# Half of the normalized gate half by a Strassen level on x in float16, with y's scaling and o's loads moved

## The chip, the cores and the metric

The kernel runs on one core of a Trainium2 chip. The metric is the time of one execution on the device in microseconds (us); lower is better. A core has five engines that run their own instruction streams and meet at semaphores: TensorE (PE, matrix products; PEld is its weight load), VectorE (DVE), ScalarE (ACT), GpSimd (POOL) and SyncE (SP), which here only issues DMAs. Matmul results go to eight banks of 128 x 512 float32, from which VectorE and ScalarE fetch them.

## The reference, cut to what matters

Two branches read the same x of 2048 tokens by 1024 and are mixed by a gate per token:

```python
qkv = (x @ wqkv)            # 1024 x 3072: 32 heads of 32, q, k and v
logits = q . k[pos - 2*w] * 32**-0.5      # w = 0..7, masked where pos - 2*w < 0
o = softmax(logits) . v[pos - 2*w]
a = o @ wo                  # 1024 x 1024
z = gelu(x @ w_in)          # 1024 x 3584, tanh form
z1, z2 = z[:, :1792], layernorm(z[:, 1792:])
b = (z1 * (w_sp @ z2 + b_sp)) @ w_out     # w_sp 2048 x 2048, w_out 1792 x 1024
g = sigmoid(x . gate_w)
out = g * a + (1 - g) * b
```

All inputs are bfloat16.

## The kernel before

Almost all of the on-chip memory is one arena, cut by hand into regions whose tenants follow one another. x is held transposed (`xT`, 1024 rows on 8 x 128 partitions, 2048 tokens). The long matrix products are TensorE's stream, in this order:

- x's first transposes and 11 tiles of z2. A z2 tile (`z2_block`, L332) is 128 tokens by one column block of 448 (`ZC`): eight matmuls (L339) into one bank, then a gelu on ScalarE that also sums each row (L345). z2 has 16 x 4 such tiles. Column block 3 carries one column more, x times gate_w, which a small copy on ScalarE takes to `gl_s` (L348).
- q, k and v (`qkv_tile`, L739), eight groups of four heads with 16 tiles each: eight matmuls of 384 columns, a copy on ScalarE into one of three staging slots (L742), and every four tiles three DMA stores to scratch in HBM (L747). Behind group 1 stand eight z2 tiles.
- The other z2 tiles. Between them ScalarE takes squares of finished z2 rows (L797, for the variance) and the row norms of w_sp (`row_norm`, L572: the sum of absolute values of 128 rows of 2048, loaded by `load_nat`, L569). Ten row norms are spread over the q/k/v groups, 13 us apart; six stand here. VectorE makes means and variances for four tiles at a time (`stats`, L622) and normalizes z2 in place (`norm`, L631), to float16.
- z1: 64 tiles of the same kind (L836, gelu L839), stored to scratch.
- The mixing product w_sp @ z2 in 16 groups (`g_group`), by one Strassen level: seven products of eight matmuls of 448 columns in float16 (L853) in place of eight products. The operands' sums and differences are made ahead by VectorE; the results are combined in three banks and in copies on ScalarE (`fork`, L875; `keep`, L863 and L865). Behind them come the product with z1 (L908), the norm of y (`y_norm`, L696), a power of two as scale (`y_power`, L701) and the scaling to float16 (`y_scale`, L709, VectorE), and a store of y to scratch (`store_y`, L652).
- o @ wo and y @ w_out, by one Strassen level each, and the gated sum.

Meanwhile VectorE computes the attention from the scratch copies of q, k and v, head group by head group: products (L362), folds (L366), the maximum over the eight positions (`soft_a`, L383), the exponentials on ScalarE (L387), and the sums with v (L402, L408). Each group's q and k are loaded by `load_qk` (L415), its v by `load_v` (L419), and its result o is stored by `store_o` (L423).

The order of all side work is written out when the program is built, by a planner. `Beat` holds an estimate of TensorE's time (`now`, advanced by `beat.run` with each matmul's columns) and of VectorE's (`vector`); `beat.at(t, fn)` issues `fn` into the engines' streams when `now` passes t, and the attention's steps are issued `lead` ahead of the time at which VectorE should reach them. In the mixing stage three lists take spare work: `beside_fork` and `beside_copy` at two places of ScalarE's stream in each group, and `behind_mult` on VectorE. The engines run each stream strictly in order, so a wait of one instruction holds what stands behind it.

SP issues the DMAs in the order of the program; a DMA whose source is not ready holds those behind it. When the last attention group is done, `attended` (L473) stores o, loads wo, takes o's norm (`o_norm`, L499), and plans the transposing loads of o (`plan_heads`, `load_heads`, L492), o's scale and the sums of wo. wo's own norm is taken in eleven chunks (`wo_norm`, L670), whose loads follow one another from ScalarE's queue, in the mixing stage.

## Time and profile before

| | |
|---|---|
| time, median of 3 runs | 679.54 us (678.07 to 680.69) |
| the profiled execution | 679.48 us |
| its span, first to last instruction | 677.7 us |
| TensorE busy | 670.1 us, 99% |
| VectorE busy | 537.5 us, 79% |
| ScalarE busy | 381.1 us, 56% |
| GpSimd busy | 15.5 us, 2% |
| granted TensorE clock, mean | 1.0 |

The stages of TensorE, from the timeline: first z2 tiles to 24.8 us, q/k/v to 203.5 (group 0 to 45.6), the other z2 tiles to 271.9, z1 to 369.2, mixing to 541, wo to 584, w_out to 677. VectorE's attention runs from 55.27 to about 464.

The lines of the profile are read as follows. A group line names a line of the kernel, the engine, the operation, output and input tiles and their shapes, the count, the busy time in us and the mean of one in ns, and, behind the last bar, the idle time just before these instructions with what ended most of it. A line of the waits gives the waiting engine and instruction, what released it, and then the total time, the number of waits and the longest. A line of the timeline gives the start, the duration, the engine, the line and the operation; a bracket at its end holds the wait before it.

### The profile page before, as it was taken

The page shows a single profiled execution, that of the slowest core. Times are in us where ns is not written, and L with a number is a line of the kernel's source. Part 1 is how long each engine was busy: PE and PEld are TensorE (multiplying, and loading weights), DVE is VectorE, ACT ScalarE, POOL GpSimd, SP SyncE. Part 2 cuts the span into 40 slices and gives each one's busy share as a digit, 9 for nine tenths or more (in the row PEclk, how much of TensorE's full clock was granted, in tenths as well). Part 3 has the DMA queues.
Part 4 walks back from the last instruction along what each step waited for, and adds up shares of the span by engine and source line. Part 5 has one row for each costly group of instructions (what it writes and reads, how often), then busy time and mean ns, then how long its engine had stood idle before and what let it go on. Part 6 is the DMA issues. An engine that isn't in the chain of part 4 may idle for free.

```text
span 677.7 us, 9532 instructions
## 1 busy us (share of the span) xinstructions
PE 670.1 (99%) x3587; PEld 392.5 (58%) x3587; DVE 537.5 (79%) x588; ACT 381.1 (56%) x714; POOL 15.5 (2%) x68
## 2 busy tenths in 40 slices
PE   8999999999999999999999999999899999999997
PEld 4568688888885555555555555555455544444443
DVE  1007799999999999999999999997369587954745
ACT  4334646455645985979953666667555574522121
POOL 0000000000000002010100000000000000000000
PEclk9999999999999999999999999999999999999999
DMA  8979869988879754267545555949966699485211
GB/s 233 179 151 281 222 163 289 236 221 219 199 195 241 231 191 175 83 204 251 169 158 176 138 133 148 270 109 248 250 161 164 166 235 251 78 172 144 59 62 63
DMA packets 230734, 123.92 MB, mean 183 GB/s; under 512 B 191008, under 2 KB 217248, under 8 KB 230688
## 3 DMA queue, kind: packets, MB, share of 16 engines
q1 hardware_dynamic: 229104, 121.21, 68.6%
q10 hardware_dynamic: 1584, 2.10, 0.9%
q8 instruction: 28, 0.46, 0.3%
q14 instruction: 18, 0.15, 0.1%
HBM read 63.97 MB, written 37.82 MB: 150 GB/s over the span
## 4 chain that ended last, share of the span: by engine, by line
PE 95%; DMA 2%; SPq 2%; ACT 0%; issue 0%; DVE 0%; ACTq 0%
PE ps L853 36%; PE ps L739 18%; PE ps L339 11%; PE ps L836 11%; PE sd L739 6%; PE seed L853 6%; PE sd L339 4%; PE sd L836 4%; SPq L492 1%; DMA o_d<-arena 1%; DMA arena<-in_B_w_in_dram 1%; DMA y_d<-arena 0%; ACT arena L670 0%; SPq L720 0%; DVE arena L1011 0%
## 5 line engine op out<-in xcount | busy, mean ns | idle before, releaser
L853 PE MATMUL ps<-arena 128*128 128x448 f16 (+1 forms) x1296 | 264.4, 363 | 1.9 <-ACT arena L865 1.9
L853 PEld LDWEIGHTS <-arena 128*128 128x128 f16 x1512 | 147.8, 98 | 156.8 <-issue 2.6
L739 PEld LDWEIGHTS <-arena 128*128 128x128 bf16 x1024 | 141.7, 138 | 24.9
L739 PE MATMUL ps<-arena 128*128 128x384 bf16 x768 | 130.0, 326 | 0.0
L362 DVE TENSOR_TENSOR arena<-arena 128x8192 bf16<-128x8192 bf16 x16 | 70.8, 4422 | 43.9 <-DMA arena<-k_d 43.6
L339 PE MATMUL ps<-arena 128*128 128x448 bf16 (+1 forms) x384 | 77.9, 357 | 0.8 <-DMA arena<-in_B_w_in_dram 0.8
L742 ACT CAST arena<-ps 128x384 bf16<-128x384 f32 x96 | 45.1, 481 | 58.7 <-PE ps L739 58.7
L339 PEld LDWEIGHTS <-arena 128*128 128x128 bf16 x512 | 50.3, 99 | 47.3 <-issue 2.0
L836 PEld LDWEIGHTS <-arena 128*128 128x128 bf16 x512 | 50.0, 98 | 46.6
L366 DVE TENSOR_TENSOR arena<-arena 128x4096 bf16<-128x4096 bf16 (+1 forms) x64 | 74.1, 1158 | 2.0
L836 PE MATMUL ps<-arena 128*128 128x448 bf16 x384 | 75.4, 352 | 0.0
L402 DVE TENSOR_TENSOR arena<-arena,att_A 128x8192 bf16<-128x8192 bf16 x16 | 70.7, 4421 | 0.2
L853 PE MATMUL seed<-arena 128*128 128x448 f16 (+1 forms) x216 | 47.8, 363 | 0.0
L739 PE MATMUL sd<-arena 128*128 128x384 bf16 x256 | 46.8, 326 | 0.0
L408 DVE TENSOR_TENSOR arena<-arena 128x4096 bf16<-128x4096 bf16 x16 | 36.6, 2289 | 0.3
L345 ACT ACTIVATE arena<-ps 128x448 bf16<-128x448 f32 x48 | 26.2, 554 | 17.6 <-PE ps L339 17.3
L572 ACT ACTIVATE arena<-arena 128x2048 bf16<-128x2048 bf16 x16 | 30.8, 1922 | 8.1 <-DMA arena<-in_B_w_sp_dram 8.1
L1075 ACT ACTIVATE arena<-ps,omr 128x512 f32<-128x512 f32 x24 | 16.5, 688 | 32.7 <-PE ps L853 32.7
L839 ACT ACTIVATE arena<-ps 128x448 bf16<-128x448 f32 x48 | 25.1, 557 | 17.1 <-PE ps L836 16.0
L865 ACT ACTIVATE arena<-ps,bt 128x448 f32<-128x448 f32 x32 | 20.3, 634 | 21.9 <-PE ps L853 20.0
L1011 DVE SCALAR_TENSOR_TENSOR arena<-seed,omr,arena 128x512 bf16<-128x512 f32 x8 | 6.0, 750 | 32.7 <-PE seed L853 32.7
L696 ACT ACTIVATE arena<-arena 128x896 bf16<-128x896 bf16 x32 | 30.3, 946 | 1.0 <-DVE arena L908 0.5
(136 smaller groups left out, 602.3 us busy)
## 6 DMA issues: line engine op xcount, KB each, us to landing
arena<-in_B_w_sp_dram SPq DMA_DIRECT2D x16, 512.0 KB, 6.1
arena<-k_d SPq DMA_DIRECT2D x8, 960.0 KB, 7.1
arena<-v_d SPq DMA_DIRECT2D x8, 960.0 KB, 5.3
z_d<-arena SPq DMA_DIRECT2D x16, 448.0 KB, 3.1
arena<-z_d SPq DMA_DIRECT2D x16, 448.0 KB, 4.0
y_d<-arena SPq DMA_DIRECT2D x16, 448.0 KB, 3.6
arena<-in_A_wqkv_dram SPq DMA_DIRECT2D x24, 256.0 KB, 5.6
arena<-in_B_w_in_dram SPq DMA_DIRECT2D x6, 896.0 KB, 5.8
```

What stands on the lines that cost most here:

```text
L339: nc.tensor.matmul(ps[:, 0:N], xT[:, kt, i * P:(i + 1) * P], w2[:, kt, ZC * c:ZC * c + N], start=(kt == 0), stop=(kt == KT - 1))
L345: nc.scalar.activation(z2[:, i, ZC * c:ZC * (c + 1)], ps[:, 0:ZC], ACT.Gelu_apprx_tanh, accum_out=s1[:, 4 * i + c:4 * i + c + 1])
L362: TT(prod.rearrange("p (w j c) -> p w j c", w=W, j=8, c=C), in0, in1, ALU.mult)
L366: return lambda: TT(pv[:, :, 0:n], pv[:, :, 0:n], pv[:, :, n:2 * n], ALU.add)
L402: TT(prod.rearrange("p (w j d h) -> p w j d h", w=W, j=8, d=DH, h=HG), in0, in1, ALU.mult)
L408: return [(4.4, mul), (2.3, lambda: TT(p3[:, 0:4, :], p3[:, 0:4, :], p3[:, 4:8, :], ALU.add)), (1.2, lambda: TT(p3[:, 0:2, :], p3[:, 0:2, ...
L572: nc.scalar.activation(waste, slot, ACT.Abs, accum_out=l1[:, a:a + 1])
L696: nc.scalar.activation(waste, g_ring[n % 4][:, r], ACT.Abs, accum_out=yl[:, k:k + 1])
L739: nc.tensor.matmul(ps[:, 0:3 * C].rearrange("p (t c) -> p t c", t=3), lhsT, wgt[:, :, kt, :], start=(kt == 0), stop=(kt == KT - 1))
L742: nc.scalar.copy(st[:, j % 4, :].rearrange("p (t d h) -> p t d h", t=3, h=HG), ps[:, 0:3 * C].rearrange("p (t h d) -> p t d h", t=3, h=HG))
L836: nc.tensor.matmul(ps[:, 0:512 if whole and kt == 0 else ZC], xT[:, kt, i * P:(i + 1) * P], _sub_ap(w1, kt * ZC, [[1, 512 if whole and kt ...
L853: nc.tensor.matmul(ps[:, 0:c1 - c0], w[:, k, :], v[:, k, c0:c1], start=(first and k == 0), stop=(k == K - 1), skip_group_check=True)
```

## The change

z2's column blocks 2 and 3 are no longer computed tile by tile. For each of eight units of 256 tokens (`Tokens`) and the 896 columns of these two blocks, `z2_group` computes 2 x 2 blocks of results by one Strassen level: seven products of four matmuls of 449 columns (128 tokens by 512 rows of x; the 449th column is gate_w's). Three results of products are kept on ScalarE (`z2_keep`), VectorE makes two sums of them and a bank, two gelus read banks at once, and the other two (`z2_late`) read the sums in the next group, behind its fifth product; GpSimd takes the gate's column from there. The last-named two gelus stand before the third keep on ScalarE.

The operands of these products have to be float16. x is converted in place, each unit by a power of two: VectorE sums its absolute values (`x_abs`), a matmul with ones adds the partitions (`x_scales`), and VectorE multiplies (`x_convert`) and makes sums and differences (`x_sums`). The sums of the first four units are taken before group 0 of q/k/v, those of the others inside it, and the second scale matmul stands behind the fourteenth tile of group 0. Groups 1 to 7 of q/k/v and all z1 tiles read the converted x; their copies and gelus undo the scale. w_in's blocks are loaded in quarters (`load_d`), normed and scaled on ScalarE (`d_norm`, `d_convert`), and subtracted on VectorE (`d_sum`).

The eight groups stand inside q/k/v group 3, ahead of tiles 0, 3, 6, 9, 12 and 14 and behind the last. Of the other z2 tiles, three stand behind group 0, two ahead of group 3 and sixteen behind group 7; the eight behind group 1 go.

Moved or resized beside it: thirteen early row norms in place of ten, issued 5.9 us apart from the end of group 3, into two slots and in place; two staging slots for q/k/v in place of three; the first group's q and k loaded in halves; the maximum in `soft_a` by three halvings; squares with each of the last 16 z2 tiles' rows, and means and variances for eight tiles at a time; wo's norm in the z1 stage. In the mixing stage y's scale power follows the first group of a unit and the scaling is done by ScalarE in the second one (`y_scale_beside`), in two halves. After the attention, o's loads are planned later and apart, wo's load behind the first of them, and wo's scaling and sums behind that.

```diff
-L1_EARLY = 10
+L1_EARLY = 13
...
-    stage_slots = [reg(R_OFF + 29952 + r * 1536, 1536).rearrange("p (j c) -> p j c", j=4) for r in range(3)]
+    stage_slots = [reg(R_OFF + 29952 + r * 1536, 1536).rearrange("p (j c) -> p j c", j=4) for r in range(2)]
...
+    def x_abs(u):
+        nc.vector.tensor_reduce(xl[:, u:u + 1], tokens[u].raw, AX.XY, ALU.add, apply_absolute_value=True)
+
+    def x_cast(u0, u1):
+        nc.vector.tensor_copy(rs_n[:, u0:u1], xl[:, u0:u1])
+
+    def powers(src, scale, inv):
+        nc.vector.tensor_scalar(scale, src, 2.0 ** -30, 2.0 ** -13, ALU.max, ALU.mult)
+        nc.vector.tensor_scalar(scale.bitcast(U32), scale.bitcast(U32), EXPO, EXPO, ALU.bitwise_and, ALU.bitwise_xor)
+        nc.vector.tensor_scalar(inv.bitcast(U32), scale.bitcast(U32), EXPO, EXPO, ALU.bitwise_and, ALU.bitwise_xor)
+        nc.vector.tensor_scalar(inv, inv, 0.5, None, ALU.mult)
+
+    def x_scales(u0, u1):
+        ps = psum.tile([P, 512], F32, name="ps", tag="ps")
+        nc.tensor.matmul(ps[:, 0:u1 - u0], rows_one, rs_n[:, u0:u1], start=True, stop=True)
+        powers(ps[:, 0:u1 - u0], xs[:, u0:u1], xinv[:, u0:u1])
+
+    def x_convert(u):
+        nc.vector.tensor_scalar(tokens[u].whole, tokens[u].raw, xs[:, u:u + 1], None, ALU.mult)
+
+    def x_sums(u):
+        v = tokens[u]
+        TT(v.s1, v.a21, v.a22, ALU.add)
+        a11, a21 = [a.rearrange("p (r k) t -> p r k t", r=2) for a in (v.a11, v.a21)]
+        TT(v.s3, a11, a21, ALU.subtract)
+        TT(v.s2, v.s1, v.a11, ALU.subtract)
+        TT(v.s4, v.a12, v.s2, ALU.subtract)
...
+    def load_d(q):
+        h, c = q // 2, 2 + q % 2
+        sync.dma_start(d_raw[:, q, :, 0:ZC], win_v[:, 4 * h:4 * h + 4, FH + ZC * c:FH + ZC * (c + 1)])
+
+    def d_norm(q):
+        nc.scalar.activation(x_waste, d_raw[:, q], ACT.Abs, accum_out=dl[:, q:q + 1])
+
+    def d_total():
+        nc.vector.tensor_reduce(dsc, dl, AX.X, ALU.add)
+        nc.vector.tensor_copy(rs_n[:, 8:9], dsc)
+        beat.on_vector(0.3)
+
+    def d_scale():
+        ps = psum.tile([P, 512], F32, name="ps", tag="ps")
+        nc.tensor.matmul(ps[:, 0:1], rows_one, rs_n[:, 8:9], start=True, stop=True)
+        powers(ps[:, 0:1], dsc, dinv)
+        nc.vector.tensor_scalar(zinv, xinv, dinv, None, ALU.mult)
+        beat.on_vector(0.9)
+
+    def d_convert(q):
+        nc.scalar.activation(d_h[:, q], d_raw[:, q], ACT.Copy, scale=dsc)
+
+    def d_sum(m):
+        out_, a, b = ((r1, m12, m11), (r3, m22, m12), (r2, m22, r1), (r4, m21, r2))[m]
+        TT(out_, a, b, ALU.subtract)
+        beat.on_vector(1.1)
...
+    def z2_keep(ps):
+        out = z2_snaps[z2_kept[0] % 5]
+        z2_kept[0] += 1
+        nc.scalar.copy(out, ps[:, 0:DN - 1])
+        return out
+
+    def z2_product(ps, w, v, first):
+        for k in range(4):
+            lhsT = w[:, k // 2, k % 2, :] if len(w.shape) == 4 else w[:, k, :]
+            nc.tensor.matmul(ps[:, 0:DN - 1], lhsT, v[:, k, 0:DN - 1], start=(first and k == 0), stop=(k == 3),
+                             skip_group_check=True)
+        beat.run(4 * (DN - 1))
+
+    def z2_late(i, src, scale):
+        z2_out(src[:, 0:ZC], i, 3, scale)
+        nc.gpsimd.tensor_scalar(gl_s[:, i:i + 1], src[:, ZC:ZC + 1], scale, None, ALU.mult)
+
+    z2_wait = []
+
+    def z2_group(u):
+        v = tokens[u]
+        scale = zinv[:, u:u + 1]
+        pa, pd = [psum.tile([P, 512], F32, name="ps", tag="ps") for _ in range(2)]
+        z2_product(pa, v.a11, m11, True)
+        pb = seeded.tile([P, 512], F32, name="seed", tag="sd")
+        nc.scalar.copy(pb[:, 0:DN - 1], pa[:, 0:DN - 1])
+        z2_product(pd, v.s1, r1, True)
+        p5 = z2_keep(pd)
+        z2_product(pa, v.s2, r2, False)
+        u2 = z2_keep(pa)
+        z2_product(pb, v.a12, m21, False)
+        z2_out(pb[:, 0:ZC], 2 * u, 2, scale)
+        z2_product(pa, v.s3, r3, False)
+        while z2_wait:
+            z2_late(*z2_wait.pop(0))
+        u3 = z2_keep(pa)
+        TT(p5, p5, u3, ALU.add)
+        z2_product(pd, v.s4, m22, False)
+        TT(u2, u2, pd[:, 0:DN - 1], ALU.add)
+        beat.on_vector(1.3)
+        z2_product(pa, v.a22, r4, False)
+        z2_out(pa[:, 0:ZC], 2 * u + 1, 2, scale)
+        z2_wait.extend([(2 * u + 1, p5, scale), (2 * u, u2, scale)])
...
-        nc.vector.tensor_reduce(att_m[:, :, 0, :], L[:].rearrange("p (a w n) -> p a n w", a=2, w=W), AX.X, ALU.max)
+        TT(att_m[:], L4[:, :, 0:4, :], L4[:, :, 4:8, :], ALU.max)
+        TT(att_m[:, :, 0:2, :], att_m[:, :, 0:2, :], att_m[:, :, 2:4, :], ALU.max)
+        TT(att_m[:, :, 0:1, :], att_m[:, :, 0:1, :], att_m[:, :, 1:2, :], ALU.max)
...
         store_o(NG - 1)
-        load_wo()
         o_norm(NG - 1, reg(A_OFF + 8192, 2048).rearrange("p (j c) -> p j c", j=NJ))
         prep["attended"] = True
         t = max(beat.now, beat.vector)
-        plan_heads(0, t + 5.0, 3.0)
-        plan_heads(1, t + 11.0, 3.0)
-        beat.at(t + 5.0, o_total)
+        plan_heads(0, t + 7.0, 3.0)
+        beat.at(t + 10.5, load_wo)
+        plan_heads(1, t + 16.0, 3.0)
+        beat.at(t + 6.0, o_total)
         behind_mult.append((t + 14.0, 0.0, o_matmul))
         behind_mult.append((t + 15.0, 0.9, o_power))
+        behind_mult.append((t + 18.0, 2.45, lambda: heads_sums(0)))
         for m in range(4):
-            behind_mult.append((t + 10.0, 0.75, lambda m=m: wo_scale(m)))
-        behind_mult.append((t + 13.5, 2.45, lambda: heads_sums(0)))
+            behind_mult.append((t + 24.0, 0.75, lambda m=m: wo_scale(m)))
         for m in range(2):
-            behind_mult.append((t + 13.5, 1.25, lambda m=m: wo_sum(m)))
+            behind_mult.append((t + 24.0, 1.25, lambda m=m: wo_sum(m)))
...
+    def y_scale_beside(u, r):
+        nc.scalar.activation(y_units[u % 2][:, :, r], g_units[u % 2][:, :, r], ACT.Copy,
+                             scale=ys[:, 2 * u + r:2 * u + r + 1])
+        if r == 1:
+            soon(("y", u), lambda: y_done(u))
...
-        st = stage_slots[stg[0] % 3]
-        nc.scalar.copy(st[:, j % 4, :].rearrange("p (t d h) -> p t d h", t=3, h=HG),
-                       ps[:, 0:3 * C].rearrange("p (t h d) -> p t d h", t=3, h=HG))
+        st = stage_slots[stg[0] % 2]
+        nc.scalar.activation(st[:, j % 4, :].rearrange("p (t d h) -> p t d h", t=3, h=HG),
+                             ps[:, 0:3 * C].rearrange("p (t h d) -> p t d h", t=3, h=HG),
+                             ACT.Copy, scale=1.0 if g == 0 else xq)
...
     for j in range(NJ):
         qkv_tile(0, j)
-
+        if j == 1:
+            x_scales(0, 4)
+        if j % 2 == 1 and j < 8:
+            x_convert(j // 2)
+            converted[j // 2] = True
+            x_sums(j // 2)
+            x_abs(4 + j // 2)
+        if j == 9:
+            x_cast(4, 8)
+        if j == 11:
+            pt = psum.tile([P, 4, P], BF, name="pt", tag="ps")
+            nc.tensor.transpose(pt[:, 0, 0:KT], gw_r[:], ident[0:KT, 0:KT])
+            for h in range(2):
+                nc.scalar.copy(d_raw[:, 2 * h + 1, :, ZC], pt[:, 0, 4 * h:4 * h + 4])
+        if j == 13:
+            x_scales(4, 8)
+            for u in range(4, 7):
+                x_convert(u)
+                converted[u] = True
+    x_convert(7)
+    converted[7] = True
+    x_spread()
+    for i in (3, 6, 7):
+        z2_tile(i, 1)
+    for u in range(4, 8):
+        x_sums(u)
+
+    t0 = beat.now
+    for q in range(4):
+        beat.at(t0 + 0.3 * q, lambda q=q: load_d(q))
+        beat.at(t0 + 15.0 + 2.5 * q, lambda q=q: d_norm(q))
+    beat.at(t0 + 25.5, d_total)
+    beat.at(t0 + 29.0, d_scale)
+    for q in range(4):
+        beat.at(t0 + 31.0 + 1.9 * q, lambda q=q: d_convert(q))
+        beat.at(t0 + 37.0 + 1.2 * q, lambda q=q: d_sum(q))
     sync.dma_start(bsp_r[:], B_b_sp.rearrange("(a t) -> a t", t=P))
...
+
+    def early_norms():
+        t = beat.now
+        for n in range(L1_EARLY):
+            beat.at(t + 5.9 * n, lambda n=n: load_nat(n, nat_early[n % 2]))
+            beat.at(t + 5.9 * n + 8.5, lambda n=n: row_norm(n, nat_early[n % 2]))
 
     for g in range(1, NG):
         if g + 1 < NG:
             load_wg(g + 1)
+        if g == 3:
+            for i in (4, 5):
+                z2_tile(i, 1, wake=True)
         for j in range(NJ):
-        if g == 1:
-            for i in range(8, 16):
-                z2_tile(i, 0)
...
+            if g == 3 and j in (0, 3, 6, 9, 12, 14):
+                z2_group((0, 3, 6, 9, 12, 14).index(j))
+            qkv_tile(g, j, g != 3)
+        if g == 3:
+            z2_group(6)
+            z2_group(7)
+            while z2_wait:
+                z2_late(*z2_wait.pop(0))
+            early_norms()
...
+    load_w1(0)
     load_nat(L1_EARLY, nat_late[0])
-    t = beat.now
+    load_nat(L1_EARLY + 1, nat_late[1])
     for n in range(2):
-        beat.at(t + 6.0 + 15.0 * n, lambda n=n: load_rows(0, n))
-    beat.at(t + 10.0, lambda: load_w1(0))
-    beat.at(t + 30.0, lambda: load_w1(1))
+        beat.at(t + 8.0 + 10.0 * n, lambda n=n: load_rows(0, n))
+    beat.at(t + 14.0, lambda: load_w1(1))
...
-        if i % 4 == 3:
+        if i % 8 == 7:
             beat.at(beat.now + 4.0, lambda i=i: stats(i))
-            for ii in range(i - 3, i + 1):
-                beat.at(beat.now + 8.0, lambda ii=ii: norm(ii))
...
+    for i in range(8, 16):
+        for c in range(2):
             z2_tile(i, c)
-        n = L1_EARLY + (i - 3) // 2
-        if 3 <= i and n < 16:
-            if i % 2 == 1:
-                if n + 1 < 16:
-                    load_nat(n + 1, nat_late[(n + 1 - L1_EARLY) % 2])
-                row_norm(n, nat_late[(n - L1_EARLY) % 2], junk.rearrange("p (n s) -> p n s", n=2))
-            else:
-                squares()
+        n = L1_EARLY + (i - 8) // 2
+        if i % 2 == 1 and n < 16:
+            row_norm(n, nat_late[(n - L1_EARLY) % 2])
+            if n + 2 < 16:
+                load_nat(n + 2, nat_late[(n + 2 - L1_EARLY) % 2])
+        squares()
...
+    beat.at(t + 6.0, lambda: load_wo_chunk(0))
+    for m in range(11):
+        beat.at(t + 12.0 + 7.0 * m, lambda m=m: wo_norm(m))
...
-        spare(beside_fork)
+        if n % 2 == 1 and n > 1:
+            y_scale_beside((n - 3) // 2, 0)
+        else:
+            spare(beside_fork)
         product(pd, v.s1, t1, f0, f1, True)
         p5 = keep(pd, None)
         product(pa, v.s2, t2, f0, f1, False)
         u2 = keep(pa, lo)
         product(pb, v.a12, b21, f0, f1, False)
         nc.scalar.copy(g[:, 0, 0], pb[:, 0:ZC])
-        spare(beside_copy)
+        if n % 2 == 1 and n > 1:
+            y_scale_beside((n - 3) // 2, 1)
+        else:
+            spare(beside_copy)
...
+        if fb == 0 and n > 0:
+            y_power(n // 2 - 1)
```

More of the change, by code (lines that the diff above doesn't have):

```diff
@@ L110, in warm_up @@
     def warm_up(n):
-        for r in range(2):
-            pw = seeded.tile([P, 512], F32, name="pw", tag="sd")
-            for _ in range(n // 2):
-                nc.tensor.matmul(pw[:], warm[:, 0:P], warm, start=True, stop=True)
+        pw = [seeded.tile([P, 512], F32, name="pw", tag="sd") for _ in range(2)]
+        for r in range(n):
+            nc.tensor.matmul(pw[r % 2][:], warm[:, 0:P], warm, start=True, stop=True)
+    rs_b = sm.tile([P, 512], BF, name="rs_b")
     ident = sm.tile([P, P], BF, name="ident")
@@ L325, in turn, with z2_tile, z2_block @@
             nc.vector.tensor_copy(dst, src)
-    def z2_tile(i, c):
-        z2_block([(i, c)])
-    def z2_block(blocks, ahead=0):
-        banks = [bank() for _ in blocks]
+    def z2_tile(i, c, wake=False):
+        z2_block([(i, c)], wake=wake)
+    converted = [False] * NU
+    def z2_block(blocks, ahead=0, wake=False):
+        banks = [seeded.tile([P, 512], F32, name="sd", tag="sd") if wake else bank() for _ in blocks]
         for kt in range(ahead):
```

146 lines of the change are left out of this document (87 added, 59 removed).

## The prediction

> **What bounds the kernel now.** I read the page's busy shares first, then the waits of TensorE, then the timeline around its one wait, then the groups with their shapes kept apart.
>
> ```profile
> PE 670.1 (99%) x3587; PEld 392.5 (58%) x3587; DVE 537.5 (79%) x588; ACT 381.1 (56%) x714; POOL 15.5 (2%) x68
> ```
> ```profile
> PE ps L853 <- ACT arena L865: 1.9, 1, 1.9
> PE pw L114 <- DVE arena L108: 1.2, 1, 1.2
> PE ps L339 <- DMA arena<-in_B_w_in_dram: 0.8, 1, 0.8
> ```
> Those three lines are all that TensorE ever waits for: it streams from 6 us to the end with one hole of 1.9 us. So a matmul taken away is worth its full time, and any new wait of TensorE costs its full length. In the chain of waits, 24 matmuls of 448 columns take 4.54 us, 0.189 each; 24 of 384 take 3.90, 0.1625 each. The hole:
>
> ```profile
> 471.06 9.64 SPq L492 DMA_TRANSPOSE arena<-o_d  x2
> ...
> 480.81 1.03 SPq L652 DMA_DIRECT2D y_d<-arena  x2
> ...
> 483.80 0.53 ACT L896 CAST arena<-seed 128x448 bf16<-128x448 f32 x1 [3.29 <-DMA y_d<-arena]
> ...
> 486.32 6.21 PE L853 MATMUL ps<-arena 128*128 128x448 f16 x32 [1.94 <-ACT arena L865]
> ```
> Two transposes of o hold SP's queue for 9.64 us, y's stores stand behind them, ScalarE's copy waits for the stores, and TensorE for ScalarE.
>
> The prices that I use, with shapes kept apart:
>
> ```profile
> L863 ACT COPY arena<-ps 128x448 f32<-128x448 f32 x16 | 8.5, 532 | 11.7 <-PE ps L853 11.7
> L865 ACT ACTIVATE arena<-ps,bt 128x448 f32<-128x448 f32 x32 | 20.3, 634 | 21.9 <-PE ps L853 20.0 <-DVE arena L408 0.9 <-DVE arena L609 0.5
> L383 DVE TENSOR_REDUCE att_m<-att_L 128x64 f32<-128x512 f32 x8 | 8.5, 1056 | 0.3 <-POOL att_L L377 0.3
> L120 DVE TENSOR_REDUCE both<-ident 128x8 f32<-128x128 bf16 x1 | 0.3, 286 | 0.3 <-POOL ident masks.py:199 0.3
> L622 DVE TENSOR_REDUCE mean<-s 128x4 f32<-128x16 f32 x4 | 0.6, 161 | 0.0
> ```
> ```profile
> 221.75 0.54 ACT L345 ACTIVATE arena<-ps 128x448 bf16<-128x448 f32 x1
> 222.18 0.21 ACT L345 ACTIVATION_READ_ACCUMULATOR arena<-ps 128x1 f32 x1
> 222.27 0.55 ACT L345 ACTIVATE arena<-ps 128x448 bf16<-128x448 f32 x1
> ```
> Gelus with an accumulator start 0.52 apart when queued. A per-partition operand costs 0.1 more (L865 against L863).
>
> **Part 1, the matmuls.** z2's column blocks 2 and 3 took 16 x 2 x 8 = 256 matmuls; eight groups of 7 products x 4 take 224. 32 x 0.189 = -6.05. Added: three tiny matmuls (x's and w's scale sums), 96 more 449th columns and two 512-wide starts, about +0.3.
>
> **Part 2, x's scale: a new wait early on TensorE.** VectorE, idle until 55.27 before, now makes |x| sums (eight reductions of 128x2048 bf16), casts and sums. The second scale matmul stands in TensorE's queue after tile 13 of q/k/v group 0, behind the last reduction. TensorE starts group 0 at 24.8 (timeline) and is there at 24.8 + 14 x 1.30 + 0.2 = 43.2. VectorE starts at 27.65 (after tile 1's matmul), does four small operations (0.2 apart in L518 to L520: 0.8), then four rounds of convert (0.78, L528), four sums of 512 (1.48, L529 to L532) and one reduction, then a cast (0.3 with its waits). The trace has no reduction of 2048: from L622 to L120 an element adds (286 - 161)/112 = 1.12 ns, so 161 + 2032 x 1.12 = 2.43 us; by L383, (1056 - 161)/496 = 1.80 ns, 3.8 us. I take 2.4, since L120 is contiguous bf16 as x is, and L383 strided float32. Rounds of 4.65 end at 27.65 + 0.8 + 18.6 + 0.3 = 47.4: a wait of +4.2. Bounds: at half L120's slope 1.3 us, nothing; at L383's, 9.8. [...]
>
> Four z2 tiles move behind this stage at no price. First attention now waits for x's sums of units 4 to 7 (4 x 1.48) and for later q and k: TensorE is out of group 0 near 50, halved loads land near 58, against 55.27.
>
> **Part 3, the eight Strassen groups.** A product is 4 matmuls, 0.758 us. In the built order ScalarE does per group: copy to the seed, keep p5, keep u2, gelu of the seed bank, the previous group's two late gelus, keep u3, last gelu. Product 7 accumulates into the bank that u3's copy reads, so it waits for that copy; only product 6 stands between. In g_group the same place has a product of 1.51 us and no gelus ahead. In time from the group's start: product 4 ends 3.03, ScalarE begins 0.20 later (its starts against product ends in the timeline), 3.23; three gelus of about 0.61 (0.52 + 0.09) to 5.06; copy 0.53 to 5.59; TensorE could have gone at 6 x 0.758 = 4.55. Wait 1.08. Group 0 has no late gelus, so 7 x 1.1 = 7.7. Besides, one exponential with its table loads (1.28 each, L387) falls between groups 2 and 3, its reload inside group 3, +1.0; one norm of o (1.9, L499) just before group 6, +0.8. Sum +9.5. Bounds: without operand price and collisions 7 x 0.8 = 5.6, less if ScalarE issues faster, 4; with 1.9 per group (each accumulator read at its full 0.21, sources in SBUF dearer, GpSimd's column copy late) and the collisions, 16. VectorE's two additions per group (0.62 each, L869) end before the late gelus need them: queued work ahead is a 4.42 product at most, and a group with its three q/k/v tiles lasts 9.2.
>
> **Part 4, ScalarE after q/k/v.** z2's last 16 tiles (24.3 us of TensorE) now carry 16 gelus (0.61), eight squares (1.69 apart), three row norms (1.91) and one exponential (3.1): 9.8 + 13.5 + 5.7 + 3.1 = 32.1, and the first row norm waits for a load queued behind q, k, stores and w_in. Eight banks let ScalarE lag by 7 x 1.516 = 10.6. By my count with the load landing 10.5 after the stage starts, two tiles wait, 1.4 + 1.7: +3, bounds 0 (landing at 7.5, where the row norm's turn comes) and 6 (landing at 13). The z1 stage then has 83 us of ScalarE work (64 gelus, eight squares, w_out and wo norms) in 97: the lag goes down.
>
> **Part 5, transfers.** Thirteen row-norm loads (0.5 MB) stand 5.9 us apart in groups 4 to 7 where they stood 13 apart. DMA share was 0.67 to 1.02 in 100 to 200 us, mean 0.88; a load is worth 512 KB / 330 GB/s = 1.6 us of it, so (1.6/5.9 - 1.6/13) = +0.15: about 1.0 with two stage slots instead of three. +1, bounds 0 and 5. The other moved DMAs (four quarter loads of w_in for two halves, two more q/k halves, eleven wo chunks from ScalarE's queue in the z1 stage) stand where the queue had gaps.
>
> **Part 6, mixing.** o's loads issue when its store has landed (5.16 us in the chain), transposes first, wo's 2 MB (13.2) later, so SP is not held, and y's stores pass: -1.9; bounds -1.9 and +3 (another store caught). The wo sums come later by some 15 us, hidden by VectorE's idle time: it is busy 13.9, 6.6, 19.3, 13.2 of 20 from 460 to 540, 27 idle. VectorE's additions, 16 x 0.54 + 4 x 1.05 + 2 for scales + 3 for the later start, less 1.4 x 7 for y's scaling, come to 8. If that cover were gone, wo's products would wait for the rest. y's scaling on ScalarE (2 x 1792 elements, 1.72 each as L797) ends u3 at 9.05 of a group where product 7 comes at 9.08: +0.3, bounds 0 and 2.
>
> **Sum** against the profiled execution (span 677.7, 679.48 with what lies around it; the median is 679.54): 679.5 - 6.05 + 0.3 + 4.2 + 9.5 + 3 + 1 - 1.9 + 0.3 = 689.8.
>
> **Rivals.**
> (a) ScalarE does not hold the groups: if gelus issued 0.25 us sooner each, product 7 would find its bank free. Then 689.8 - 9.5 = 680.3, no change. Against: the order is written out, and 0.52 is measured at a full queue. It decides at 0.1 us of wait per group: below that, with the collisions gone, the total is under 682.9.
> (b) All new waits hide, by TensorE's bank depth and a cheap reduction: 679.5 - 6.05 + 0.3 - 1.9 = 671.9, faster. Against: both waits are in TensorE's own order, no bank helps.
> (c) DMA is the bound in groups 4 to 7: stores land late, ScalarE waits for its two slots with q/k/v's copies behind it. At a share 8% above capacity over 83 us, +6.6: 695.4 in place of +1. For: slices at 1.0 already; against: 1.09 is seen in single stretches without a wait.
> (d) The wait in part 2 slows the clock. In the first 9 us of the trace a 448-column matmul takes 0.37, then 0.19; the hole of 1.94 us at 486 slowed nothing. If 4.2 idle us bring the slow pace back for as long as some 18 matmuls (3.4 us), it costs 1.7: 691.5. [...]
>
> **How the numbers follow.** The sum's own case 0.55, (a) 0.13, (b) 0.17, (c) 0.09, (d) 0.06. A measurement tells about 0.5%, 3.4 us, from no change. Faster is (b), 0.17; same is (a) and a little of the sum's low end, 0.15; slower the rest, 0.68. Terms at their low ends together give 680; at two high ends, near 700. (b) is not one time: with one of its waits left at its low end it lies up to 676. The range is 675 to 699, leaving the rest of (b) and a tail out; the likeliest case alone spans 683 to 697.
>
> **What would show it.** A wait of TensorE on VectorE's cast (about 4, once, near 43 us) and reductions of 2.4 us; seven waits of products on ScalarE's keep, about 1.1 each, between 100 and 180 us; waits of z2 and z1 tiles on gelus after the eighth group of q/k/v; no wait of ScalarE for y_d near 480; 32 fewer large matmuls at 0.189. The forecast is wrong if TensorE runs through the groups without a wait, or if reductions are under 1.3 us.

## The result and the profile after

The changed kernel takes 737.16 us (median of 4 runs, 735.46 to 742.33) against 680.12 before: 1.085 times, with a 95% interval of 1.081 to 1.090. The forecast was 689.8, with a range of 675 to 699. The sign was right, the size was not: +57 in place of +10.

The profiled execution is the slowest of the four, 742.33 us with a span of 740.4. First the page's busy shares and its row of the granted clock, after the change:

```profile
PE 684.7 (92%) x3558; PEld 392.4 (53%) x3558; DVE 578.0 (78%) x667; ACT 447.4 (60%) x757; POOL 37.7 (5%) x84
...
PEclk9999979999999999999899999999999999999999
```

TensorE was busy 99% of the span and is busy 92%. It also executes 32 large matmuls fewer and is nevertheless busy 14.6 us longer: in two slices the clock's row shows 0.7 and 0.8. VectorE has 40 us more work, ScalarE 66. Then TensorE's waits, of which there were three lines before:

```profile
PE ps L455 <- ACT arena L449: 11.0, 7, 2.5
PE ps L1034 <- ACT arena L1037: 6.0, 4, 4.3
PE sd L373 <- ACT arena L896: 5.3, 2, 4.9
PE ps L893 <- ACT arena L896: 3.8, 3, 3.0
PE ps L373 <- ACT arena L382: 3.3, 2, 2.7
PE ps L1051 <- ACT arena L1063: 3.3, 3, 2.2
PE ps L1034 <- ACT arena L382: 3.1, 2, 1.6
PE ps L399 <- DVE rs_n L389: 3.1, 1, 3.1
PE ps L1051 <- DVE arena L674: 2.9, 1, 2.9
PE ps L1051 <- ACT seed L1075: 2.9, 1, 2.9
PE sd L373 <- ACT arena L382: 2.3, 1, 2.3
PE ps L893 <- DVE yl L392: 2.1, 1, 2.1
```

Seen one after the other in the timeline, the holes of more than 0.1 us are 51.1 us together, 2.7 before. By place:

| place | holes, us | term of the prediction |
|---|---|---|
| x's second scale matmul (46.6) | 3.1 | +4.2 |
| w_in's scale and the two z2 tiles ahead of group 3 (86 to 109) | 8.0 | part of +0.3 |
| the Strassen groups (128 to 192) | 11.6 | +9.5 |
| q/k/v groups 4 to 7 (255 to 275) | 3.8 | +1 |
| last z2 tiles and first z1 tiles (301 to 320) | 8.7 | +3 |
| z1 (339 to 385) | 6.2 | 0 |
| mixing and wo (427 to 603) | 9.0 | -1.9 and +0.3 |

Next comes the clock. The trace records eight stretches at half clock, 34.1 us in all. TensorE is busy in 29.2 of them, so they cost 14.6. By an estimate from this place, every hole also costs some 0.16 more than its idle time:

```profile
138.31 1.70 PE L455 MATMUL ps<-arena 128*128 128x449 f16 x8
140.98 0.93 PE L455 MATMUL ps<-arena 128*128 128x449 f16 x4 [0.98 <-ACT arena L449]
```

Matmuls overlap: these start 0.193 us apart, and each counts as busy for 0.354. Eight of them need 8 x 0.193 = 1.54 us until the next one could start, but the last one counts as busy to 1.70. So the idle time of a hole is measured from 0.16 us too late; 31 more holes make 5.0. Together 48.4 + 14.6 + 5.0 - 5.3 (the matmuls saved, as measured below) = 62.7, as much as the spans differ.

What the clock's record shows is seen in busy times of TensorE in stretches of 3.4 us (columns: stretch, length, TensorE's busy time and matmuls, clock, DMA share, GB/s):

```profile
297.00:300.40 3.40, 1.51 (x8) 1.00 0.27 63
300.40:303.80 3.40, 1.67 (x8) 1.00 0.91 237
...
150.25:153.65 3.40, 1.34 (x9) 1.00 1.00 303
153.67:157.07 3.40, 3.40 (x13) 0.50 0.43 98
157.10:160.50 3.40, 3.40 (x21) 1.00 0.00 0
```

A stretch with 1.89 us idle is followed by full clock; one with 2.06 by a whole stretch at half. In that one 13 matmuls run, in the next one of the same length 21.

A caution for all times below. The record of full clock begins 9.7 us behind the start in the trace before and 10.3 in the one after. `mended` runs the same matmuls as the change up to x's first scale matmul; its trace has that matmul at 25.39 us, the change's at 27.58: 2.2 us that no edit explains, taken here as chance at the start. Thirteen runs of the kernel before lie between 676.7 and 681.3. A difference of 2 us between two kernels means little by itself.

### The profile page after: what moved, and what is told of

The parts are those of the page before. It is cut to its first block, busy times and chain, and to the rows that moved or that the text cites. A ratio compares the mean times of both kernels' runs of the same rounds, so it can differ in the third digit from the quotient of the medians.

```text
span 740.4 us, 9583 instructions
## 1 busy us (share of the span) xinstructions
PE 684.7 (92%) x3558; PEld 392.4 (53%) x3558; DVE 578.0 (78%) x667; ACT 447.4 (60%) x757; POOL 37.7 (5%) x84
## 5 line engine op out<-in xcount | busy, mean ns | idle before, releaser
L1051 PE MATMUL ps<-arena 128*128 128x448 f16 (+1 forms) x1296 | 267.5, 366 | 9.0 <-ACT arena L1063 3.3
L1051 PEld LDWEIGHTS <-arena 128*128 128x128 f16 x1512 | 148.4, 98 | 166.6 <-issue 11.2
L893 PEld LDWEIGHTS <-arena 128*128 128x128 f16 (+1 forms) x1024 | 142.4, 139 | 36.1 <-issue 11.6
L893 PE MATMUL ps<-arena 128*128 128x384 bf16 x800 | 142.8, 335 | 6.0 <-ACT arena L896 3.8
L1034 PE MATMUL ps<-arena 128*128 128x448 bf16 x384 | 77.7, 357 | 9.1 <-ACT arena L1037 6.0
L1034 PEld LDWEIGHTS <-arena 128*128 128x128 f16 x512 | 50.7, 99 | 59.5 <-issue 14.9
L896 ACT ACTIVATE arena<-ps,yl 128x384 bf16<-128x384 f32 x88 | 49.1, 585 | 43.1 <-DMA v_d<-arena 21.5
L455 PE MATMUL ps<-arena 128*128 128x449 f16 x192 | 41.2, 356 | 11.6 <-ACT arena L449 11.0
L1051 PE MATMUL seed<-arena 128*128 128x448 f16 (+1 forms) x216 | 47.8, 363 | 0.0
L373 PEld LDWEIGHTS <-arena 128*128 128x128 f16 (+1 forms) x256 | 25.9, 102 | 37.4 <-issue 17.2
L373 PE MATMUL ps<-arena 128*128 128x448 bf16 x184 | 39.3, 363 | 3.8 <-ACT arena L382 3.3
L893 PE MATMUL sd<-arena 128*128 128x384 bf16 x224 | 41.0, 326 | 0.0
L455 PEld LDWEIGHTS <-arena 128*128 128x128 f16 x224 | 22.0, 98 | 34.3 <-issue 14.9
L1037 ACT ACTIVATE arena<-ps,yl 128x448 bf16<-128x448 f32 x48 | 29.0, 640 | 14.6 <-DMA z_d<-arena 10.3
```

The lines of the kernel that those rows point to most:

```text
L373: nc.tensor.matmul(ps[:, 0:N], x[:, kt, i * P:(i + 1) * P], _sub_ap(w2, kt * W2P + ZC * c, [[1, N]]), start=(kt == 0), stop=(kt == KT - 1) ...
L455: nc.tensor.matmul(ps[:, 0:DN - 1], lhsT, v[:, k, 0:DN - 1], start=(first and k == 0), stop=(k == 3), skip_group_check=True)
L893: nc.tensor.matmul(ps[:, 0:3 * C].rearrange("p (t c) -> p t c", t=3), lhsT, wgt[:, :, kt, :], start=(kt == 0), stop=(kt == KT - 1))
L896: nc.scalar.activation(st[:, j % 4, :].rearrange("p (t d h) -> p t d h", t=3, h=HG), ps[:, 0:3 * C].rearrange("p (t h d) -> p t d h", t=3, ...
L1034: nc.tensor.matmul(ps[:, 0:512 if whole and kt == 0 else ZC], xh[:, kt, i * P:(i + 1) * P], _sub_ap(w1, kt * ZC, [[1, 512 if whole and kt ...
L1051: nc.tensor.matmul(ps[:, 0:c1 - c0], w[:, k, :], v[:, k, c0:c1], start=(first and k == 0), stop=(k == K - 1), skip_group_check=True)
```

## The experiments

### Each suspected place by itself

**The order on ScalarE in the Strassen groups.** The third keep gets a slot of its own and stands ahead of the late gelus.

```diff
-        out = z2_snaps[z2_kept[0] % 5]
+        out = z2_snaps[r]          # p5: u % 2, u2: 2 + u % 2, u3: 4
...
         z2_product(pa, v.s3, r3, False)
+        u3 = z2_keep(pa, 4)
         while z2_wait:
             z2_late(*z2_wait.pop(0))
-        u3 = z2_keep(pa)
```

> The third keep of a group of z2 products gets a slot of its own and stands ahead of the two late gelus on ScalarE; nothing else changes. Theory 1 (ScalarE's order in the groups costs what its holes show): TensorE's eight holes in the groups (11.6 us together in the trace of the change) fall to under 1.5 us, the two stretches of half clock that begin at 129.8 and 153.7 us (3.4 us each, so 1.7 each) go, and the time falls by about 13 us from 737 to 724. Rival (what is gained in the groups is lost again, since VectorE's attention, not TensorE, sets when q/k/v's groups and the mixing stage go on): the holes go but the time stays within 4 us of 737.

725.6 us (1.068 times the kernel before, 1.064 to 1.072): 11.6 us of the 57 by moving one copy and giving it a slot. The groups' holes fall from 11.6 to 1.4:

```profile
L452 PE MATMUL ps<-arena 128*128 128x449 f16 x192 | 40.0, 354 | 1.4 <-ACT arena L446 0.8 <-ACT seed L468 0.6
```

The old order was forced by the ring: the third keep of a group overwrote the slot that the late gelus, and GpSimd, still had to read. GpSimd made two of the eight holes 2.5 us long (last section).

**The Strassen level undone.** The same tiles at the same places from the same float16 operands, as plain products:

```diff
-        z2_product(pa, v.a11, m11, True)
...
+        for r, (w1, w2_) in enumerate(((v.a11, v.a12), (v.a21, v.a22))):
+            for c, (b1, b2) in enumerate(((m11, m21), (m12, m22))):
+                ps = psum.tile([P, 512], F32, name="ps", tag="ps")
+                for h, (w, b) in enumerate(((w1, b1), (w2_, b2))):
+                    for k in range(4):
+                        nc.tensor.matmul(ps[:, 0:n], w[:, k, :], b[:, k, 0:n], ...
+                z2_out(ps[:, 0:ZC], 2 * u + r, 2 + c, scale)
```

> The change with the Strassen level of z2 undone and all else kept: the same 2 x 2 tiles per unit at the same places, from the same float16 x and w_in, as four tiles of eight matmuls; no sums of x or w_in, no keeps, no additions. 32 more matmuls of 448 (+6.05 us). Theory 1 (the level loses more than it saves): the group holes (11.6) and two stretches of half clock (3.4) go, and the time is 737 + 6 - 15 = 728. Rival (the level's waits cover others that would come in their place, or the attention sets the pace): 741 to 744.

724.1 us (1.066, 1.062 to 1.069): 13 us faster than with the level, with 32 matmuls more. It cannot be told from the level with its keep moved (725.6), so the level by itself, mended, gains nothing that shows here.

**w_in's scale.** The planner is told of more VectorE time, so that the powers come ahead of an attention product.

```diff
     def d_total():
         nc.vector.tensor_reduce(dsc, dl, AX.X, ALU.add)
         nc.vector.tensor_copy(rs_n[:, 8:9], dsc)
-        beat.on_vector(0.3)
+        beat.on_vector(4.0)
```

> The planner is told that VectorE is busy longer at w_in's sum, so that the powers for w_in's scale stand ahead of the attention product (4.4 us, itself waiting for a late load of k) and not behind it; nothing is left out. Theory 1 (that one place in VectorE's order holds ScalarE's four conversions, these the copies of q/k/v, and these TensorE's banks): the waits of 2.14, 0.39 and 4.93 us at 98.9, 101.8 and 108.7 us go, so do 10 us of half clock that follow them, and the time falls by 10 to 12 us to about 726. Rival (the four conversions of 1.8 us are too much for ScalarE wherever they start): the bank waits stay at 4 us or more and the time is above 732.

The chain that it is to break, in the timeline after the change (VectorE, then ScalarE):

```profile
94.31 4.43 DVE L499 TENSOR_TENSOR arena<-arena 128x8192 bf16<-128x8192 bf16 x1 [3.42 <-DMA arena<-k_d]
98.65 0.15 DVE L392 TENSOR_SCALAR yl<-ps 128x1 f32<-128x1 f32 x1
```
```profile
99.03 1.80 ACT L437 ACTIVATE arena<-arena,yl 128x1800 f16<-128x1800 bf16 x1 [8.62 <-DVE yl L393]
```

The power needs 0.15 us; it comes 12 us after its matmul (86.1), since it stands behind a product that waits for k. ScalarE waits 8.62 us in order, q/k/v's copies behind it. The run took 731.7 us (1.077, 1.072 to 1.082): half of what was expected. The waits of 2.14 and 4.93 are gone, but a bank wait of 3.33 stays ahead of group 3, and the holes there fall from 8.0 us to 4.4. So VectorE's order accounts for about half. What is left stands behind the four conversions of 1.8 us among the copies and behind one copy that waits 1.87 us for v's store; the run does not separate these two.

**x's second scale matmul** one z2 tile behind group 0:

```diff
-        if j == 13:
-            x_scales(4, 8)
...
+    z2_tile(3, 1)
+    x_scales(4, 8)
```

> The change with x's second scale matmul, and the conversions that follow it, one z2 tile behind group 0 in place of behind its fourteenth tile. Theory (TensorE waits there for VectorE's last sum of absolute values, 3.05 us, and pays 1.7 more for the stretch at half clock behind it): 737 to about 732.5. Rival (group 1 then waits for the conversions, or the attention starts later and something behind waits for it): 736 or above.

732.6 us (1.080, 1.076 to 1.083), 4.6 less and as expected: the hole of 3.05 is gone and so is the stretch at half clock that began at 47.8.

**wo's reordering in HBM** moved into the mixing stage:

```diff
-    beat.at(t + 40.0, order_wo)
...
+    for h in range(HG):
+        beat.at(beat.now + 12.0 + 10.0 * h, lambda h=h: order_wo(h))
```

> The change with one edit: the reordering of wo from HBM to HBM (four DMAs, 2 MB) goes from 40 us behind group 7 of q/k/v into the mixing stage. In the kernel before that due time lay in the z2 stage, in the change it lies in the z1 stage, where these DMAs stand ahead of z1's store at 342.5, which lands 12.7 us later; ScalarE waits 8.65 and TensorE 4.34 for it. Theory: that hole and most of the half clock behind it go, 737 to about 730. Rival (the 1.4 MB of q and k that are loaded at the same time delay the store): the hole stays at 3 us or more, 735 or above.

The line that says `t + 40.0` is the same in both kernels, but the stage behind t became 44 us shorter, so the four DMAs moved from the z2 stage into z1's. In the timeline after the change:

```profile
336.37 6.04 SPq L708 DMA_DIRECT2D wop_d<-in_A_wo_dram  x4
...
342.52 5.32 SPq L1042 DMA_DIRECT2D z_d<-arena  x2
...
355.29 0.63 ACT L1037 ACTIVATE arena<-ps,yl 128x448 bf16<-128x448 f32 x1 [8.65 <-DMA z_d<-arena]
```

732.2 us (1.079, 1.074 to 1.083), 5 us faster where 7 were expected; the hole of 4.34 is gone. It was nowhere in the prediction.

**The last z2 tiles.** Five squares in place of eight there, the row norms later:

```diff
-        n = L1_EARLY + (i - 8) // 2
-        if i % 2 == 1 and n < 16:
+        n = L1_EARLY + (i - 11) // 2
+        if i % 2 == 1 and i >= 11:
...
-        squares()
+        if i % 2 == 0 or i == 15:
+            squares()
...
-            if square[0] < 16 and i % 3 == 2:
+            if square[0] < 16 and i % 2 == 1:
```

> The change with five squares in place of eight among the last 16 z2 tiles, the three late row norms two rows of tiles later, and the other eleven squares in the first 22 z1 tiles. Theory (ScalarE has 32 us of work in these 24 and stands 5 us for the first norm's load): the holes of 8.7 us between 301 and 320 fall below 3, 737 to about 730. Rival (the work comes back as waits of z1 tiles for gelus, since ScalarE is near full there too): 734 or above.

724.1 us (1.067, 1.063 to 1.070): 13 us, twice the expectation. No hole is left from 272 to 322; the squares that went to z1 gave back 3.5 us of holes there (1.87, 1.05, 0.58), but z1's worst hole also shrank, from 4.34 to 3.12. The excess is not shown to come from this edit: its trace has 20.5 us at half clock in place of 34.1, and none of the stretches that went lay at the mended place.

**The third staging slot** back outside group 3:

```diff
-        st = stage_slots[stg[0] % 2]
+        st = stage_slots[stg[0] % (2 if g == 3 else 3)]
...
```

> The change with the third staging slot of q/k/v back outside group 3 (its place holds x's last sum and a keep there; that sum is made in group 3). Theory (ScalarE's copies wait 21.5 us in all for a slot's stores to land, and TensorE 3.8 of it in groups 4 to 7): these holes fall below 1 us, the time by 3 to 6 us to about 733. Rival (the transfers themselves are the limit there, thirteen norm loads 5.9 us apart on top of q/k/v's): the copies wait as long for the third slot, 736 or above.

733.8 us, but 727.8 to 738.6 in four runs (1.081, 1.074 to 1.088): not told from the change. In its trace the holes of groups 4 to 7 are 1.44 us in place of 3.8, which is in line with the theory; the time doesn't prove it.

### The mixing part alone, on the kernel before

> The kernel before with the mixing stage's part of the change alone: o's loads later and apart, wo's scaling and sums behind them, wo's norm in the z1 stage, y scaled by ScalarE. The prediction's terms for it are -1.9 and +0.3: 678. Theory 1 (the 9 us of waits that the change shows in the mixing stage come from an attention that ends 97 us later, at 563 in place of 466): no new wait here, 676 to 681. Rival (y's scaling on ScalarE and wo's late sums make these waits themselves): holes of 2 to 3 us before the y groups' third products and at the first product with wo, 684 to 690.

683.8 us against 678.1 (1.007, 1.005 to 1.010). The theory falls: the part makes a wait by itself. In its timeline (VectorE and ScalarE; the last line is TensorE's):

```profile
400.52 4.42 DVE L402 TENSOR_TENSOR arena<-arena,att_A 128x8192 bf16<-128x8192 bf16 x1
...
406.97 0.17 DVE L703 TENSOR_SCALAR ys<-ys 128x2 uint32<-128x2 uint32 x1
...
407.17 1.79 ACT L714 ACTIVATE arena<-arena,ys 128x1792 f16<-128x1792 bf16 x1 [5.36 <-DVE ys L703]
...
409.28 0.64 ACT L874 ACTIVATE arena<-ps,bt 128x448 f32<-128x448 f32 x1
...
409.96 2.40 PE L862 MATMUL ps<-arena 128*128 128x448 f16 x6 [4.91 <-ACT arena L874]
```

y's power, 0.5 us of small operations, is behind an attention product; ScalarE waits for it in order, and the keep that frees TensorE's bank is behind the scaling. Next the same part with y scaled by VectorE:

```diff
-        if n % 2 == 1 and n > 1:
-            y_scale_beside((n - 3) // 2, 0)
-        else:
-            spare(beside_fork)
+        spare(beside_fork)
...
+        if fb == 0 and u > 0:
+            beat.at(beat.now + 0.5, lambda u=u: y_finish(u - 1))
```

> The kernel before with the mixing stage's part alone, but y scaled by VectorE as before: only o's and wo's later loads and sums and wo's norm in the z1 stage are left. The run with the whole part was 5.7 us slower than before, with a wait of 4.91 us behind ScalarE's y scaling. Theory 2 (ScalarE stands in order before the scaling until VectorE, which is behind an attention product of 4.4 us, has made the power): no such hole, and the hole of 1.9 us at 486 goes too: 675 to 678. Rival (wo's or o's new places cost it): 682 to 685.

675.5 us (ten runs), 0.997 times the kernel before (0.995 to 0.999). By the two ratios y on ScalarE costs 1.0%, 7 us, and o's and wo's later loads gain 2, as the term of -1.9 said. This is the only run that beats the kernel before, by 0.3%. That is no more than the chance at the start, but the times of both kernels fall into two clusters (675.0 to 675.7 and 677.3 to 678.1 here, 676.7 to 677.4 and from 678.8 there), and each of these lies about 1.5 us lower than its counterpart; the hole of 1.94 is gone from the trace.

### The clock by itself

```diff
+        if g > 0 and j in (5, 11):
+            for _ in range(1 + holes[0] % 7):
+                nc.scalar.copy(waste, ps[:, 0:384])
+            holes[0] += 1
+            pt = psum.tile([P, 512], F32, name="pt", tag="ps")
+            nc.tensor.matmul(pt[:, 0:1], ident[:], waste[:, 0:1], start=True, stop=True)
```

> The kernel before with 14 holes put into TensorE's stream in q/k/v groups 1 to 7: behind tiles 5 and 11 of each stands a tiny matmul that reads what one to seven extra copies of a bank on ScalarE leave (about 0.5 us each). Expected holes of 1.4 to 4.4 us, 41 us together. Theory (a stretch of 3.41 us of the clock's record in which TensorE stood idle for 2.0 us or more is followed by one at half clock, as the change's trace shows for 2.06 us and not for 1.93): holes under 2.0 us cost their length alone, those above cost up to 1.7 us more where they do not straddle two stretches, in sum about 8 x 1.7: 732. Rival (the clock follows something else, such as the load since the start or the other engines): no stretch at half clock, 719.

```profile
PE pt L758 <- ACT arena L755: 36.9, 14, 4.0
```

730.6 us (1.077, 1.072 to 1.083). The span grew by 50.7: 36.9 of holes, and 13.5 for the 30.7 us at half clock, in which TensorE is busy for 27.1. These make 50.4; the 14 ends of holes at 0.16 would add 2.2, and full clock that began 2.9 us sooner than before takes some 1.7 away. Of the eight holes of 2.9 us and more, six are followed by half clock; two (2.94 and 2.99) are not. These two straddle a boundary of the record's grid and leave 1.67 and 1.87 idle in one stretch. The rival falls.

### All places mended

> The change with the places mended that its trace shows: the third keep ahead of the late gelus in a slot of its own; w_in's quarter blocks loaded, normed and scaled in group 0 already, the second scale matmul of x one z2 tile behind group 0, the two late z2 tiles from ahead of group 3 there too; three staging slots outside group 3; fewer squares and later row norms in the last z2 tiles; wo's reordering in HBM in the mixing stage; y's scaling on ScalarE about one half group later. Theory (the waits are local, each mended where it stands): of 51 us of holes and about 17 of half clock some 15 and 5 stay: 737 - 48 = 689, 683 to 697. Rival (VectorE, 40 us busier and with its attention ending 97 us later, bounds the change as a whole, and mended waits come back as waits for VectorE): over 705.

702.6 us (1.037, 1.032 to 1.042): between the theory (683 to 697) and its rival (over 705). The new places made holes of their own: 0.80, 3.26 and 2.82 us where gate_w's column and w_in's quarters were now needed before they had landed, 3.58 in z1. The second try moves these again:

```diff
+    for q in range(4):
+        load_d(q)
+    for i in (6, 7, 4, 5):
+        z2_tile(i, 1)
...
+        beat.at(t0 + 4.0 + 2.2 * q, lambda q=q: d_norm(q))
+    beat.at(t0 + 13.5, d_total)
+    beat.at(t0 + 19.0, d_scale)
...
+        beat.at(t0 + 25.0 + 2.2 * q, lambda q=q: d_convert(q))
+        beat.at(t0 + 31.0 + 1.3 * q, lambda q=q: d_sum(q))
```

> The run with all places mended, with its own new waits mended in turn: w_in's quarters loaded behind group 0 and normed, scaled and subtracted spread over groups 1 and 2 (their early loads made waits of 0.80, 3.26 and 2.82 us), six squares among the last z2 tiles and ten in z1 (a hole of 3.58). Left as they are: ScalarE in the groups (5.8), an exponential at the start of mixing (2.4), wo's last sums (2.9). Theory (each wait is local): 702.6 - 10.5 - 1.7 = 690. Rival (ScalarE's and VectorE's added work, 66 and 40 us, makes new waits wherever the old ones go): 697 or above.

696.6 us (1.027, 1.024 to 1.030), at the rival's edge (697) and not at the theory's 690. Its waits:

```profile
PE ps L1047 <- DVE arena L682: 4.8, 1, 4.8
PE ps L1030 <- ACT arena L1033: 4.0, 5, 1.6
PE ps L1047 <- DVE arena L672: 3.2, 1, 3.2
PE ps L453 <- ACT seed L469: 2.6, 2, 1.8
```

The first and third stand at the first products with wo; 10.2 us at half clock begin there. VectorE's last operation of the attention now ends at 521 us, 147 behind the start of mixing; in the kernel before it ended 94 behind it. Whether that is VectorE's added work was the last question:

```diff
-                for took, fn in pv_steps(g - 1, 0):
+                for took, fn in pv_steps(g - 1, 0) if g < NG - 1 else []:
...
-                for took, fn in pv_steps(g - 1, 1):
+                for took, fn in pv_steps(g - 1, 1) if g < NG - 1 else []:
```

> The second mended kernel (696.6 us) with 17 us of VectorE's work taken away: the sums with v of the seventh of the eight head groups are left out (that group's o is not computed). Theory (VectorE's 40 us of added work end the attention late, and with it o's and wo's loads, so that the first products with wo wait 4.84 and 3.18 us and 10.2 us at half clock follow): these holes go, 696.6 - 8 - 5 = 683 to 685. Rival (the planned distances between the attention's end and wo's loads and sums make them, whatever VectorE has to do): they stay, 694 or above.

684.7 us (1.011, 1.006 to 1.015), as the theory said: both waits are gone, so is every stretch at half clock.

```profile
PE ps L1030 <- ACT arena L1033: 3.7, 5, 1.6
PE ps L453 <- ACT seed L469: 2.6, 2, 1.8
PE ps L453 <- ACT arena L447: 2.3, 2, 1.5
PE ps L1047 <- ACT arena L1059: 1.9, 1, 1.9
```

So 12 of the 19 us that the second mended kernel still loses come from VectorE's load: with eight operations fewer (16 us of its busy time) these waits go, and the attention ends at 484. The other 7 us stay; behind the start, the waits that are left are all on ScalarE. The run leaves out one group's o, and the same cut was not made in the kernel before; there TensorE has one hole of 1.94 us and little to gain. No version with the Strassen level came below the kernel before.

## Why the prediction was wrong

**Right.** The matmuls: the 224 of the level start 0.193 us apart, 43.2 us; the 256 that they replace stood 0.189 and 0.190 apart, 48.5 us. That is -5.3 for -5.75. Part 2: the wait stands where it was said, behind VectorE's cast, 3.05 us where +4.2 was taken. The reductions took 2.28 us for 2.43 estimated. Part 3's mechanism: seven waits of the product on the third keep, 0.98 us in four groups for 1.08 predicted (its own terms give 5.59 - 4.55 = 1.04), 2.06 behind the exponential's table load, 2.47 and 2.53 behind GpSimd; with 0.64 behind the norm of o, 11.6 in all for +9.5. The -1.9 of o's loads.

**The step that failed most is rival (d).** Against the profiled execution the sum is 52 us short: the holes that are new come to 48.4 where its terms hold 16.1, the clock to 14.6 and the ends of the holes to 5 where it holds nothing. So the clock is the largest single term. Rival (d) priced the clock at 1.7 us once, with a chance of 0.06, and argued from a hole of 1.94 us that "slowed nothing". The 18 slow matmuls (3.4 us) of its condition were the author's guess: the trace before shows no slow pace behind a hole. The trace after has a stretch of 3.41 us at half clock behind this wait, and seven more; together they cost 14.6. The hole of 1.94 lies just under what had an effect: in the trace after, 1.93 us idle in one stretch of the clock's grid had none and 2.06 had one, and in `slots3` 1.97 had one.

**Costs left out.** "Three tiny matmuls" (+0.3) counted the durations of w_in's scale and not its place: VectorE's 0.15 us operation behind a product of 4.4, and behind that ScalarE, q/k/v's copies and TensorE: 8.0 of holes and two stretches at half clock. The +0.3 for y on ScalarE is the same error: it added 1.72 us of ScalarE, and left out that the scaling waits for a power made by VectorE in order; measured +7 on the kernel before. The prediction asked what stands ahead in order where TensorE waits anew, and not where ScalarE does. "Lag goes down" in z1 missed wo's reordering, whose due time hangs on a stage that the change shortened.

**Sizes.** z2's last tiles +3, in the trace 8.7, above the bound of 6: the first norm's load landed 16.9 us into the stage, not 10.5 to 13, as it stood in SP's queue behind stores of q, k and v that waited for ScalarE's late copies. Groups 4 to 7: +1, in the trace 3.8, within the bounds.

**The range** took in "two high ends" only. By the stated bounds all low ends together give 676, not the 680 that it names, and all high ends 716, so that no mixture of its terms reaches 737. The terms were also added as if independent. That they were not is argued from the runs: each hole makes TensorE later than the order of the other engines was planned for, and in both mended kernels new waits came where old ones went. That the attention, with o's norm, would end 97 us later (563 in place of 466) was in no rival; it is the largest part of what is left when the others are mended.

## What to carry to other kernels

When an operation is moved to another engine, the price is not only its duration but also the place of what it waits for in the order of the engine that makes it: look for the longest instruction that can stand ahead of each small producer. Where side work is planned against an estimate of the time, a stage that becomes shorter moves everything planned from its start into the next stage; go through those due times. And a hole of a little over 2 us cost TensorE nearly twice its length here: 2.06 and then 1.7 for the stretch at half clock, where it lay within one stretch of the clock's grid.

## What the hardware showed unexpectedly

In the trace after, the record of the granted clock goes by a fixed grid of 3.413 us: all its changes up to TensorE's end lie on whole multiples of that from 10.30, where full clock begins. Of the grid's stretches at full clock, those with 1.93 us idle or less (1.89 in the 3.40 us shown above) were followed by full clock, and all eight with 2.06 or more by half. In the trace before the largest idle time in a stretch is 1.94, followed by full clock. In `slots3` 1.97 us was followed by half clock, in `graded_holes` 1.88 by full and 2.08 by half. In a stretch of the trace after that was already at half clock, 0.65 us idle or less was followed by full clock (at 426.7), 0.93 and 2.87 by another stretch at half (at 355.0 and 105.9). Both agree with an estimate of about 1.4 us of full-clock matmuls in a stretch as the border (3.41 - 2.0 = 1.4; half of 3.41 less 0.65 to 0.93 is 1.2 to 1.4); that it is the work which is counted is argued, not shown.

GpSimd's scaling of one element per partition took 0.27 or 0.28 us in eight of 16 cases. Four took 4.1 to 4.4, each beside a bf16 product of 4.42 on VectorE, three 2.26 beside a bf16 sum of 2.29, and one 1.19 beside a sum of 1.22; each of these eight ended 0.14 to 0.17 us behind VectorE's instruction. Of the eight short ones, three ran beside nothing on VectorE and five beside a sum of 0.62 that reads a bank (L484). ScalarE's third keep, and with it TensorE, waits for it:

```profile
123.67 4.42 DVE L541 TENSOR_TENSOR arena<-arena,att_A 128x8192 bf16<-128x8192 bf16 x1
...
123.94 4.57 POOL L461 TENSOR_SCALAR gl_s<-arena,ys 128x1 f32<-128x1 f32 x2
...
128.29 0.53 ACT L449 COPY arena<-ps 128x449 f32<-128x449 f32 x1 [1.37 <-POOL gl_s L461]
...
128.88 0.93 PE L455 MATMUL ps<-arena 128*128 128x449 f16 x4 [2.47 <-ACT arena L449]
```

What makes GpSimd's instructions last as long as VectorE's is not shown.
